# A wait moved: the zero fills of a decode-attention kernel start after the first V load instead of after the output weight

## The chip, the cores, the metric

One core of one Trainium2 chip. The metric is device microseconds (us) of one execution, median over several runs. Times inside an execution are counted from the start of the profiled span, which is about 1.8 us shorter than the device time (763.0 us against 764.8 us).

## The reference

The program is the forward and backward pass of one decode step: layer norm, sliding-window attention over a cache, a gate made by a small MLP, and the gradients of everything. Only the sizes matter here.

```python
B, Sq, D = 2, 1, 512
Hq, Hkv, Sk, Dh = 32, 8, 32768, 128           # the caches are 2 x 8 x 32768 x 128, bf16
W = min(4096, max(256, Sk // 4))              # = 4096: only the last 4096 rows are attended to
k = jnp.repeat(k_cache[:, :, Sk - W:, :], rep, axis=1)
v = jnp.repeat(v_cache[:, :, Sk - W:, :], rep, axis=1)
...
_out, _vjp = jax.vjp(_f, A_x, A_k_cache, A_v_cache, ...)   # returns gradients of the WHOLE caches
```

The gradient of each cache has 32768 rows per head, and 28672 of them are zero. The kernel must write these zeros: 32 heads of 7.3 MB. Together with the 33.6 MB of real gradients, the weights and their gradients, that is 280.5 MB of writes and 45.6 MB of reads.

## The kernel before

The zero fills are DMAs that POOL issues from one tile of zeros (`zt`). They make up 227.6 of 326.7 MB. A fill needs no result, so the kernel is free to choose when fills start; it lets the first one wait for the load of the output weight `wo`.

```python
dma_load = nc.sync            # loads: SP queue
dma_store = nc.scalar         # stores of gradients: ACT queue
...
def zf(o, q, r0, nent, rows, rep=1):          # one zero fill, POOL's queue
    ...
    zs = zt[0:nent * st:st, 0:w].unsqueeze(1).to_broadcast([nent, rep, w])
    sw_fill.append(nc.gpsimd.dma_start(out=v, in_=zs))
    return r0 + nr
...
kvp = attn.enter_context(tc.tile_pool(name="kvp", bufs=1))
w12 = kvp.tile([P, NCB * DH], BF16, tag="k")              # w1 and w2 lie in the tile of K!
w1 = w12[:, 0:DK * F].rearrange("p (k f) -> p k f", k=DK)
w2 = w12[:, DK * F:DK * F + FK * D].rearrange("p (j d) -> p j d", j=FK)
...
def load(src, r, tag):
    nat = kvp.tile([P, NCB * DH], BF16, tag=tag)
    dma_load.dma_start(out=nat[:], in_=kv_of(src, r))     # 4 MB, 32 KB per partition
    return nat[:].rearrange("p (c d) -> p c d", d=DH)
...
    dma_load.dma_start(out=w1, ...)                       # 1.8 MB
    dma_load.dma_start(out=w2, ...)                       # 1.8 MB
    wo_in = dma_load.dma_start(out=wo[:], ...)            # 4 MB
    dma_load.dma_start(out=wq[:], ...)                    # 4 MB
    vnat = load(A_v_cache, 0, "v")                        # V 0
    for qi in range(ZQ - 1):
        ...                                               # 54 fills of 31 heads
    for f in sw_fill:
        tc.add_manual_dep(f.ins, wo_in.ins.name, ...)     # fills wait for wo
    ...                                                   # MLP, transposes of w1, w2, wo; q
knat = load(A_k_cache, 0, "k")                            # K 0: waits until w1, w2 are transposed
for r in range(NR):                                       # 4 rounds: scores, softmax, gradients,
    ...                                                   # store dV, load next V, store dK, load next K
...
with tc.issue_after(last.ins):
    fin = nc.sync.dma_start(out=v, in_=zs)                # the fill of the 32nd head ends the program
```

K 0 shares its tile with `w1` and `w2`, so its load is issued late, when PE has transposed both; and POOL issues its fills in order, so holding back the first holds back all.

Of the kernel before, what the change touches and what calls it, by code (L numbers as in the profile page):

```python
# [16 lines left out]
def kernel(  # L17
# [35 lines left out]
    NJ = N // P  # L53
# [14 lines left out]
    dma_load = nc.sync  # L68
# [21 lines left out]
    def zf(o, q, r0, nent, rows, rep=1):  # L90
        b, hk = divmod(q, HKV)
        nr = nent * rows * rep
        v = o[b, hk, r0:r0 + nr, :]
        w = rows * DH
        if w > ZG * DH:
            v = v.bitcast(F32)
            w //= 2
        v = v.rearrange("(r p g) d -> p r (g d)", p=nent, g=rows)
        st = 4 if nent < 16 else 1
# [3 lines that stand above are left out]
# [71 lines left out]
    wo = wts.tile([P, NJ, D], BF16, name="wo")  # L174
# [29 lines left out]
    def kv_of(t, r):  # L204
        b, h0 = rounds[r]
        return t[b, h0:h0 + NP, SK - W:SK, :].rearrange("h (k c) d -> k h (c d)", c=NCB)

    def load(src, r, tag):
        nat = kvp.tile([P, NCB * DH], BF16, tag=tag)
        dma_load.dma_start(out=nat[:], in_=kv_of(src, r))  # L210
        return nat[:].rearrange("p (c d) -> p c d", d=DH)

    with tc.tile_pool(name="pw", bufs=1) as pw:
# [9 lines left out]
        nc.vector.memset(one_row[:], 1.0)  # L223
        dma_load.dma_start(out=w1, in_=B_w1.rearrange("(p k) f -> p k f", k=DK))
        dma_load.dma_start(out=w2, in_=B_w2.rearrange("(p j) d -> p j d", j=FK))
        wo_in = dma_load.dma_start(out=wo[:], in_=A_wo.rearrange("(p j) m -> p j m", j=NJ))
        dma_load.dma_start(out=wq[:], in_=A_wq.rearrange("(p k) n -> p k n", k=DK))
        vnat = load(A_v_cache, 0, "v")
        for qi in range(ZQ - 1):
            r = 0  # L230
            whole = (P, ZR // P, 1) if qi in zlong else (P, ZG, ZR // (P * ZG))
            for n, rows, rep in zshort.get(qi, (whole,)):
                r = zf(*zparts[qi], r, n, rows, rep)
            assert r == ZR
        for f in sw_fill:
            tc.add_manual_dep(f.ins, wo_in.ins.name,
                              mybir.DependencyInfo(mybir.DependencyClass.Sync, mybir.DependencyReason.DATA))

        tp = ps_m.tile([P, DK, B], BF16, tag="m")
# [65 lines left out]
        for g0 in range(0, len(jobs), 8):  # L305
# [4 lines left out]
            j = 0  # L310
# [10 lines left out]
        for j0 in range(0, NJ, JG):  # L321
            woT = pw.tile([P, JG, DK, P], BF16, tag="woT", bufs=2)
            for half in range(2):
                tp = ps_t.tile([P, 8, P], BF16, tag="pt")
                for jj in range(8):
                    j, dk = divmod(half * 8 + jj, DK)
# [99 lines left out]

    NR = len(rounds)
    knat = load(A_k_cache, 0, "k")
    for r in range(NR):
        nc.vector.tensor_copy(out=zdo[:, :, ZO:ZO + REP], in_=heads(doT_all, r))  # L430
# [110 lines left out]
        if r + 1 < NR:  # L541
            vnat = load(A_v_cache, r + 1, "v")
# [128 lines left out]
```

## Time and profile before

| | before |
|---|---|
| device time, median of 3 (range) | 764.79 us (764.75 to 764.82) |
| profiled span | 763.0 us |
| bytes moved by DMA | 326.73 MB, mean 428 GB/s |
| busy: PE, DVE, ACT, POOL | 52%, 36%, 28%, 4% |
| end of compute; issue of the final fill | 726.7 us; 727.14 us |

The page cuts the span into 40 slices (19.1 us each). Its row DMA is the busy share of the 16 DMA engines in tenths, the row below it what they moved.

```profile
DMA  9999999999999999999999999999999999999998
GB/s 382 439 424 437 410 443 434 435 423 433 419 436 440 419 440 434 427 426 431 431 429 443 431 431 422 432 430 445 426 436 437 431 434 434 415 432 434 421 426 378
DMA packets 10973, 326.73 MB, mean 428 GB/s; under 512 B 2548, under 2 KB 2557, under 8 KB 2586
```

The engines are busy from end to end, and bytes over rate is the span: nothing that compute does matters as long as the engines have something to move. The Trainium skill ("DMA: Bandwidth & Descriptors", Where 436 GB/s comes from) puts the ceiling of the fabric at 435 GB/s; this trace runs at 431 over its long stretch, just below it.

What POOL and SP issue at the start (start, duration, queue, line, transfer; in brackets how long the engine had been idle, and what released it):

```profile
22.88 4.86 POOL L101 DMA_DIRECT2D out_dram<-zt  x8 [21.22 <-DMA wo<-in_A_wo_dram]
```

```profile
2.97 0.61 SPq L210 DMA_DIRECT2D nat<-in_A_v_cache_dram  x1
38.97 0.54 SPq L210 DMA_DIRECT2D nat<-in_A_k_cache_dram  x1
...
726.72 0.33 SPq L635 DMA_DIRECT2D out_dram<-dw  x1
727.14 0.41 SPq L640 DMA_DIRECT2D out_dram<-zt  x1
```

V 0 is queued at once, K 0 only at 38.97 us. The table of stretches gives, for each, the busy time of each engine with counts, then PE's granted clock, the DMA busy share and GB/s, the last column:

```profile
22.00:38.00 16.00, 14.18 (x171) 12.90 (x171) 4.89 (x18) 4.78 (x7) 4.86 (x8) 1.00 1.08 438
38.00:50.00 12.00, 6.93 (x74) 4.68 (x74) 5.69 (x7) 6.24 (x6) 0.00 (x0) 1.00 1.15 429
50.00:100.00 50.00, 39.02 (x364) 22.30 (x363) 19.36 (x33) 19.27 (x19) 1.74 (x3) 0.76 1.05 423
100.00:760.00 660.00, 326.25 (x3424) 191.31 (x3432) 234.37 (x399) 179.99 (x274) 24.33 (x44) 0.65 1.08 431
```

This view does not cut a packet at the edge of a stretch well (a stretch of 4 us can show 508 GB/s), so I use it for 12 us and more. For finer steps I take the trace's packet records and spread each packet's bytes evenly over its duration. From these I also make a sum that the rest leans on, the **lost time**: over steps of 1 us, the sum of (431 - rate) / 431, where 431 GB/s is the rate of the long stretch from 100 to 760 us. It says how many microseconds of full-rate transfer were not used. (The trace's packet records list the packets that a transfer is cut into, each with start, duration, size and queue.)

### The profile page before, as it was taken

Reading aid. Unit: us, or ns where it says so; the run is one execution under the profiler, and the core shown is the slowest. Engines: PE = TensorE matmul, PEld = TensorE weight load, DVE = VectorE, ACT = ScalarE, POOL = GpSimd, SP = SyncE. Lnnn points to the kernel's source line nnn. Section 1 sums busy time; section 2 is a strip of 40 time slices with the busy share of each in tenths; the row PEclk is TensorE's granted clock in tenths of the full one; section 3 lists DMA queues with packets and bytes.
Section 4 is the critical chain, followed back from the end, with each engine's and each line's share of the span. In section 5 each row is a group of like instructions: output and inputs, shape, how many; then the busy total and the mean of one; then the engine's idle time right before and its main releaser. Section 6 shows DMA issues by size and latency. Waiting matters only on the chain.

```text
span 763.0 us, 9422 instructions
## 1 busy us (share of the span) xinstructions
PE 398.6 (52%) x4127; PEld 242.3 (32%) x4136; DVE 274.7 (36%) x481; ACT 216.7 (28%) x314; POOL 32.0 (4%) x63
## 2 busy tenths in 40 slices
PE   5866973853035748640187485002644784866900
PEld 4742552420023534210055341002433443323200
DVE  4334342823012455330054555001324451665600
ACT  3253323523001145430022455000114230721600
POOL 0200000000000100000000000000000000000000
PEclk9986896766558857665579577555767595855555
DMA  9999999999999999999999999999999999999998
GB/s 382 439 424 437 410 443 434 435 423 433 419 436 440 419 440 434 427 426 431 431 429 443 431 431 422 432 430 445 426 436 437 431 434 434 415 432 434 421 426 378
DMA packets 10973, 326.73 MB, mean 428 GB/s; under 512 B 2548, under 2 KB 2557, under 8 KB 2586
## 3 DMA queue, kind: packets, MB, share of 16 engines
q0 software_dynamic: 6784, 227.55, 70.4%
q1 hardware_dynamic: 2696, 56.63, 21.1%
q10 hardware_dynamic: 1452, 41.95, 15.2%
q8 instruction: 32, 0.52, 0.3%
q14 instruction: 9, 0.07, 0.0%
HBM read 45.62 MB, written 280.50 MB: 427 GB/s over the span
## 4 chain that ended last, share of the span: by engine, by line
PE 34%; DMA 33%; DVE 12%; ACT 10%; issue 7%; ACTq 0%; DVEq 0%; SPq 0%
DMA out_dram<-nat 16%; DMA nat<-in_A_k_cache_dram 10%; PE ov L417 7%; PE tp L383 6%; DMA nat<-in_A_v_cache_dram 5%; ACT tring L150 3%; ACT p_bf L451 2%; ACT nat L150 2%; DVE nat L152 2%; PE ps L406 2%; PE s_ps L390 2%; DVE ds_bf L464 2%; PE wps L584 2%; PE dops L331 1%; DVE tring L152 1%
## 5 line engine op out<-in xcount | busy, mean ns | idle before, releaser
L383 PE MATMUL tp<-pperm,nat 128*128 128x128 bf16 x1024 | 93.3, 244 | 178.0 <-DMA nat<-in_A_v_cache_dram 146.1
L152 DVE COPY tring<-tp 128x1024 bf16<-128x1024 bf16 (+1 forms) x98 | 66.3, 689 | 192.1 <-PE tp L383 188.7
L383 PEld LDWEIGHTS <-nat 128*128 128x128 bf16 x1024 | 69.4, 109 | 198.4 <-DMA nat<-in_A_v_cache_dram 148.1
L150 ACT CAST nat<-ov 128x512 bf16<-128x512 f32 x160 | 87.7, 590 | 78.5 <-PE ov L417 57.7
L150 ACT COPY tring<-tp 128x1024 bf16<-128x1024 bf16 (+1 forms) x34 | 34.4, 1011 | 247.6 <-PE tp L383 220.6
L152 DVE CAST nat<-ov 128x512 bf16<-128x512 f32 x96 | 65.7, 690 | 69.3 <-PE ov L417 66.9
L417 PE MATMUL ov<-bd,ds_bf 128*128 128x512 bf16 x124 | 50.0, 483 | 19.0 <-issue 12.9
L101 POOL DMA_DIRECT2D out_dram<-zt x54 | 30.4, 567 | 531.3 <-DMA out_dram<-zt 510.1
L417 PE MATMUL ov<-bd,p_bf 128*128 128x512 bf16 x123 | 46.7, 447 | 5.5 <-ACT nat L150 1.4
L406 PE MATMUL ps<-t,nat 128*128 128x16 bf16 x1024 | 28.8, 173 | 18.2 <-issue 11.4
L406 PEld LDWEIGHTS <-nat 128*128 128x128 bf16 x1024 | 28.7, 103 | 21.1 <-issue 16.0
L152 DVE CAST wq<-wps 128x512 bf16<-128x512 f32 x16 | 11.0, 690 | 54.4 <-PE wps L577 54.2
L390 PEld LDWEIGHTS <-zz 128*32 128x32 bf16 x512 | 17.6, 96 | 33.6 <-issue 23.5
L150 ACT CAST wq<-wps 128x512 bf16<-128x512 f32 x16 | 9.4, 586 | 63.6 <-PE wps L577 63.6
L390 PE MATMUL s_ps<-tring,zz 128*32 128x256 bf16 x256 | 20.0, 301 | 11.2 <-ACT tring L150 7.5
L398 PE MATMUL tp<-ident_bf,p_bf 128*128 128x128 bf16 x64 | 7.5, 310 | 34.9 <-ACT p_bf L451 34.9
L390 PE MATMUL dp_ps<-tring,zz 128*32 128x256 bf16 x256 | 20.0, 319 | 7.4 <-ACT tring L150 5.0
L451 ACT ACTIVATE p_bf<-e_sb,rl 32x512 bf16<-32x512 f32 x16 | 22.8, 1423 | 3.4 <-DVE rl L448 3.3
L417 PEld LDWEIGHTS <-ds_bf 128*128 128x128 bf16 x128 | 13.4, 111 | 27.4 <-issue 25.6
L464 DVE SCALAR_TENSOR_TENSOR ds_bf<-dp_ps,delta,p_bf 32x512 bf16<-32x512 f32 x16 | 21.6, 1352 | 0.2
L417 PEld LDWEIGHTS <-p_bf 128*128 128x128 bf16 x128 | 12.8, 109 | 19.7 <-issue 16.8
L398 PEld LDWEIGHTS <-p_bf 128*128 128x128 bf16 x64 | 6.5, 144 | 35.8 <-ACT p_bf L451 35.8
(198 smaller groups left out, 465.1 us busy)
## 6 DMA issues: line engine op xcount, KB each, us to landing
out_dram<-zt POOLq DMA_DIRECT2D x23, 7168.0 KB, 98.8
out_dram<-nat ACTq DMA_DIRECT2D x8, 4096.0 KB, 41.3
nat<-in_A_v_cache_dram SPq DMA_DIRECT2D x4, 4096.0 KB, 38.4
nat<-in_A_k_cache_dram SPq DMA_DIRECT2D x4, 4096.0 KB, 39.6
out_dram<-zt POOLq DMA_DIRECT2D x2, 7072.0 KB, 68.9
out_dram<-zt POOLq DMA_DIRECT2D x3, 3584.0 KB, 93.2
out_dram<-zt SPq DMA_DIRECT2D x1, 7168.0 KB, 35.0
out_dram<-zt POOLq DMA_DIRECT2D x1, 7104.0 KB, 120.6
```

What stands on the lines that cost most here:

```text
L101: sw_fill.append(nc.gpsimd.dma_start(out=v, in_=zs))
L150: nc.scalar.copy(out=out_ap, in_=in_ap)
L152: nc.vector.tensor_copy(out=out_ap, in_=in_ap)
L331: nc.tensor.matmul(dops[0:B, :, :], lhsT=dsT_bf[:, dk, :], rhs=woT[:, :, dk, :], start=(dk == 0), stop=(dk == DK - 1))
L383: nc.tensor.transpose(tp[:, j, :], nat[:, g * CC + half * CH + j, :], pperm[:].rearrange("p b k -> p (b k)"))
L390: nc.tensor.matmul(out_ps[pr * RB:(pr + 1) * RB, half * CH * PB:(half + 1) * CH * PB], lhsT=zbuf[:, pr, o:o + RB], rhs=tT[:, :, pr, :], st ...
L398: nc.tensor.transpose(tp[:, cc, :], src[:, half * CH + cc].rearrange("r k b -> r (k b)"), ident_bf[:, :])
L406: nc.tensor.matmul(ps[:], lhsT=nat[:, g * CC + half * CH + cc, :], rhs=cols[half][:, cc, :, g, :], start=(half == 0 and g == 0 and cc == 0 ...
L417: nc.tensor.matmul(ov[:], lhsT=src[:, cc].rearrange("r k b -> r (k b)"), rhs=bd[:, gh * 4:(gh + 1) * 4, :], start=True, stop=True)
L451: nc.scalar.activation(out=p_bf[rb, :, :, pr], in_=e_sb[rb], func=ACT.Copy, scale=rl[rb, 0:1])
L464: nc.vector.scalar_tensor_tensor(out=ds_bf[rb, :, :, pr], in0=dp_c[rb], scalar=delta[rb, 0:1], in1=p_bf[rb, :, :, pr], op0=ALU.subtract, o ...
L584: nc.tensor.matmul(wps[:], lhsT=o_rows[:, j:N:NJ], rhs=ds_rows[:, :], start=True, stop=True)
```

## The change

Hold the fills back until V 0 has landed. The intent: in the first stage the loads get the engines to themselves, so V 0 is there earlier. No instruction is added, removed or reordered; the listing of both programs engine by engine differs in the one semaphore that POOL's first fill waits for.

```diff
+    kv_loads = []
+
     def load(src, r, tag):
         nat = kvp.tile([P, NCB * DH], BF16, tag=tag)
-        dma_load.dma_start(out=nat[:], in_=kv_of(src, r))
+        kv_loads.append(dma_load.dma_start(out=nat[:], in_=kv_of(src, r)))
         return nat[:].rearrange("p (c d) -> p c d", d=DH)
@@
-        wo_in = dma_load.dma_start(out=wo[:], in_=A_wo.rearrange("(p j) m -> p j m", j=NJ))
+        dma_load.dma_start(out=wo[:], in_=A_wo.rearrange("(p j) m -> p j m", j=NJ))
@@
         for f in sw_fill:
-            tc.add_manual_dep(f.ins, wo_in.ins.name,
+            tc.add_manual_dep(f.ins, kv_loads[0].ins.name,
                               mybir.DependencyInfo(mybir.DependencyClass.Sync, mybir.DependencyReason.DATA))
```

## The prediction

> **What bounds the kernel now.** The DMA engines. The page's queue table sums to 326.73 MB and the DMA row of its slices shows 9 tenths in 39 of 40 slices, mean 428 GB/s: bytes over rate is the whole 763.0 us span. The trace's packet records, summed per 20 us, give 428 to 433 GB/s from 2 us to 762 us without a hole. The Trainium skill ("DMA: Bandwidth & Descriptors", Where 436 GB/s comes from) gives a ceiling of 435 GB/s; the trace agrees. PE is busy 52%, DVE 36%, ACT 28%. Compute ends at 726.7 us; the last 35 us are stores of the output weight and the last zero fill (issued 727.14, landed 35.0 us later).
>
> **What the change does.** No instruction is added, removed or reordered; the programs' listings differ in one wait of POOL: the first fill waits for V load 0 instead of wo. Before, wo landed at 22.1 us, the first fill was issued at 22.88 us, and its first packet ran at 27.1 us. V load 0 landed at 50.8 us, sharing the engines with fills (packets of 57,344 bytes against its 32,768). Now the loads have the engines alone: w1, w2, wo, wq and V are 16.25 MB, which at 431 GB/s plus 1.7 us of start (an estimate) land at 40 to 41 us, 10 us sooner. Fills are issued then; their first packets run near 45 us, 18 us later than now.
>
> **How much is on the critical path.** Almost nothing.
> - The engines should not run dry at the hand-over. The load of K 0 waits for the transposes of w1 and w2 (last at 38.7 us) and is issued at 38.97 us, its first packet 0.2 us later. So K 0 (4.19 MB, 9.7 us alone) is queued 1 to 2 us before V drains and covers the 5 us until the first fill packet.
> - Earlier V, wq and K buy nothing: V is first read at 86.4 us, wq at 74 us, and before 155 us PE waits for no DMA but x and w1 (2.2 and 5.9 us). This stage is paced by PE, ACT and DVE; the first store of dV stays at 153 us.
> - The queues share the engines without losing throughput ("DMA: Bandwidth & Descriptors", Issuing engines are not separate DMA queues). Fills postponed by 18 us are caught up by 86 us, when K 0 has landed in both: the same bytes have then moved, and the rest finds the same backlog. The fills still end near 728 us.
>
> Reads alone ran at 433 GB/s, mixed with fills at 430: 18 us of that saves 0.1 us. Hand-over holes cost 0 to 1 us.
>
> **Prediction.** 764.9 us, range 763.9 to 766.4. Faster by over 2%: 0.01; within: 0.97; slower: 0.02.
>
> **What would show each step.** First fill issued at 40 to 42 us; issue to landing of V 0 near 38 us rather than 47.8; K 0 landed near 60 us rather than 86, still issued at 39 us; first store of dV near 153 us; DMA at 428 GB/s or more between 40 and 50 us; last software fill packet within 2 us of 728.5; final fill issued near 727. Bytes unchanged.
>
> **What would make it wrong.** K 0 issued later or slow to start, so that the engines idle until fill descriptors arrive: up to 5 us lost. Or the fills' odd sizes, apparently tuned to balance the 16 engines, fall beside other transfers and leave single engines idle at the end: 1 to 3 us. Or later loads meet a different mix and delay the compute end past what 15 us of queued stores cover.

## The result

| | before | changed |
|---|---|---|
| device time, median of 6 (range) | 764.88 us (764.75 to 765.04) | 766.93 us (766.02 to 768.00) |
| ratio, 95% interval | 1 | 1.0026 (1.0014 to 1.0039) |
| profiled span | 763.0 us | 766.2 us |
| first fill issued by POOL | 22.88 us | 43.15 us |
| K 0 issued by SP | 38.97 us | 38.95 us |
| end of compute (issue of the store of dw1) | 726.72 us | 711.02 us |
| lost time, 10 to 100 us | 0.35 us | 1.85 us |
| lost time, 100 to 760 us | -0.28 us | -0.15 us |
| lost time of the uneven end (from 758 us to the last packet) | 0.85 us | 2.40 us |

A ratio is the mean time of one kernel's fast runs over that of the other's of the same rounds, so it is not quite the ratio of the medians quoted. The change is slower by 2.05 us (0.26%), clear of the interval though well within 2%. The profiled run is the slowest of the six (768.0 us); the others' spans were 764.2 to 765.3 us.

The slices of the page after:

```profile
DMA  9999999999999999999999999999999999999998
GB/s 384 431 388 436 420 444 423 441 420 434 434 422 436 422 446 429 430 426 437 424 427 438 435 427 433 431 430 438 438 429 435 426 427 420 437 441 417 440 416 344
DMA packets 10973, 326.73 MB, mean 426 GB/s; under 512 B 2548, under 2 KB 2557, under 8 KB 2586
```

Same packets, same bytes. The **third** slice (38 to 57 us) has fallen from 424 to 388 GB/s, and the last from 378 to 344. Note that the busy share still reads 9 in the third slice. POOL, SP and the stretches after (lines of the file are two higher than before):

```profile
43.15 4.84 POOL L101 DMA_DIRECT2D out_dram<-zt  x8 [41.50 <-DMA nat<-in_A_v_cache_dram]
```

```profile
2.81 0.60 SPq L212 DMA_DIRECT2D nat<-in_A_v_cache_dram  x1
38.95 0.54 SPq L212 DMA_DIRECT2D nat<-in_A_k_cache_dram  x1
...
711.02 0.33 SPq L637 DMA_DIRECT2D out_dram<-dw  x1
713.63 0.39 SPq L642 DMA_DIRECT2D out_dram<-zt  x1
```

```profile
22.00:38.00 16.00, 14.28 (x166) 12.94 (x167) 4.84 (x17) 5.06 (x7) 0.00 (x0) 1.00 1.02 436
38.00:50.00 12.00, 8.35 (x72) 5.58 (x72) 4.83 (x6) 5.96 (x5) 4.84 (x8) 0.86 0.99 374
50.00:100.00 50.00, 37.40 (x389) 22.31 (x389) 20.93 (x35) 20.03 (x20) 1.73 (x3) 0.86 1.19 426
100.00:760.00 660.00, 322.53 (x3409) 186.89 (x3408) 233.33 (x397) 179.15 (x274) 24.25 (x44) 0.66 1.07 431
```

From 38 to 50 us the busy share is 0.99 and the engines move 374 GB/s instead of 429; from 100 us on both run at 431. The share sums the times of all packets, the 4-byte ones that end a transfer included, so it can exceed 1 (1.15 before) and does not say that every engine is at work. GB/s in steps of 1 us, from the packet records:

```
us       38  39  40  41  42  43  44  45  46  47  48  49
before  422 436 427 433 431 427 439 431 429 431 436 432
changed 433 421 294 309 366 385 368 339 299 322 391 432
```

The records also show how many packets are under way. With loads alone it is 16.0 or 16.1 in every step from 28 to 39 us of the changed run, one for each of the 16 engines, so a number below 16 means engines without work (4-byte packets left out; "again" is the second profile told of below):

```
us         38   39   40   41   42   43   44   45   46   47   48   49
before   16.0 16.6 16.2 16.4 16.4 16.1 16.4 16.3 16.2 16.1 16.4 16.3
changed  16.0 15.6 12.2 14.6 15.2 16.0 16.0 16.0 15.6 16.0 16.0 16.0
again    16.0 16.0  8.2 11.4 16.0 16.0 16.0 16.1 16.1 16.0 16.1 16.0
```

So there are two different losses. From 40 to 43 us engines do stand empty: V 0 ended on its 16 engines at 39.8 to 42.1 us, and K 0's first packet ran at about 40.3 us, 1.3 us after its issue began (records do not name the transfer; I tell K 0's packets by their length). The empty places make 0.40 of the 0.77 us lost from 39 to 43 us, and 0.78 of 1.07 us in the second profile. The rest is slow packets: V 0's of 32,768 bytes take 1.21 us each until 40 us; those that began between 40.3 and 41.3 us took 1.57 us on average, up to 1.93. From 43 to 48 us nearly all places are filled, and the packets are slow. The first packet of a fill ran at 47.95 us, and by 49 us the rate was back.

The sums close: 1.50 us more lost from 10 to 100 us and 1.55 us more at the uneven end make 3.05 us; the last packet ended 3.24 us later (765.00 against 761.76 us). That is book-keeping (the bytes are the same): it shows where time was lost. What it does not tell is why K 0 ran slowly, and whether the uneven end is a consequence or a second cause. For there is a rival: in the changed run compute ended 15.7 us earlier, the final fill was issued at 713.6 us instead of 727.1, and it mixed with other fills.

### The profile page after: what moved, and what is told of

It is laid out like the page before. It is cut to its first block, busy times and chain, and to the rows that moved or that the text cites. A ratio compares the mean times of both kernels' runs of the same rounds, so it can differ in the third digit from the quotient of the medians.

```text
span 766.2 us, 9431 instructions
## 1 busy us (share of the span) xinstructions
PE 395.2 (52%) x4136; PEld 239.2 (31%) x4136; DVE 274.3 (36%) x481; ACT 216.6 (28%) x314; POOL 31.9 (4%) x63
## 4 chain that ended last, share of the span: by engine, by line
PE 33%; DMA 32%; DVE 12%; ACT 10%; issue 6%; ACTq 0%; DVEq 0%; SPq 0%
DMA out_dram<-nat 17%; DMA nat<-in_A_v_cache_dram 9%; PE tp L385 6%; PE ov L419 6%; DMA nat<-in_A_k_cache_dram 5%; ACT tring L150 3%; ACT p_bf L453 2%; DVE tring L152 2%; ACT nat L150 2%; DVE ds_bf L466 2%; PE s_ps L392 2%; DVE nat L152 2%; PE wps L586 2%; PE ps L408 1%; PE dops L333 1%
## 5 line engine op out<-in xcount | busy, mean ns | idle before, releaser
L385 PE MATMUL tp<-pperm,nat 128*128 128x128 bf16 x1024 | 88.9, 237 | 167.3 <-DMA nat<-in_A_v_cache_dram 151.9
L385 PEld LDWEIGHTS <-nat 128*128 128x128 bf16 x1024 | 65.8, 106 | 186.6 <-DMA nat<-in_A_v_cache_dram 153.7
L419 PE MATMUL ov<-bd,p_bf 128*128 128x512 bf16 x128 | 49.5, 460 | 4.1 <-DVE nat L152 1.4
L408 PEld LDWEIGHTS <-nat 128*128 128x128 bf16 x1024 | 28.6, 102 | 20.1 <-issue 15.0
L392 PE MATMUL s_ps<-tring,zz 128*32 128x256 bf16 x256 | 19.3, 290 | 12.2 <-ACT tring L150 7.6
```

Of the source, the lines that this page charges most:

```text
L385: nc.tensor.transpose(tp[:, j, :], nat[:, g * CC + half * CH + j, :], pperm[:].rearrange("p b k -> p (b k)"))
L392: nc.tensor.matmul(out_ps[pr * RB:(pr + 1) * RB, half * CH * PB:(half + 1) * CH * PB], lhsT=zbuf[:, pr, o:o + RB], rhs=tT[:, :, pr, :], st ...
L408: nc.tensor.matmul(ps[:], lhsT=nat[:, g * CC + half * CH + cc, :], rhs=cols[half][:, cc, :, g, :], start=(half == 0 and g == 0 and cc == 0 ...
L419: nc.tensor.matmul(ov[:], lhsT=src[:, cc].rearrange("r k b -> r (k b)"), rhs=bd[:, gh * 4:(gh + 1) * 4, :], start=True, stop=True)
```

## The experiments

Theory A: the loss is made at 39 to 49 us, where K 0 is alone in the queues. Theory B: it is made at the end, because the first stage is lightened, compute ends early, the final fill starts early and the engines end unevenly. Later theories appear where they came up. Medians of before are those of the same rounds (9 or 11 runs); the others have 5 runs, or 6 where said. Every kernel gave correct results.

### Fills wait for wq, which lands between wo and V 0

```diff
-            tc.add_manual_dep(f.ins, kv_loads[0].ins.name,
+            tc.add_manual_dep(f.ins, wq_in.ins.name,
```

> All fills wait for wq (lands near 31 us) in place of V 0. Theory A (the loss of about 2 us is made at 39 to 49 us, where the load of K 0 is alone in the queues and does not run the engines at 431 GB/s): here V 0 and then fill packets (from about 36 us) lie beside the start of K 0, so there is no hole at 39 to 43 us; 764.8 to 765.3 us, 0 to 0.4 us over before. Theory B (the loss is made at the end, because compute ends some 15 us earlier, the final fill is issued early and mixes with the software fills, and the 16 engines end unevenly): the stage before is lightened nearly as much as in the change, compute ends early too, and the time is 766 to 767 us. Sub-question: if POOL's burst of eight issues slows any load (A1), the packets of V 0 at 32 to 36 us take 1.3 to 1.5 us instead of 1.213.

Measured: 764.61 us (764.51 to 764.73) against 764.79 (764.69 to 764.95); ratio 0.9997 (0.9985 to 1.0009). POOL's first issue was at 33.26 us, its first packet at 37.20. Lost from 39 to 49 us: nothing (-0.05 us); a small dip at 34 to 39 us (0.33 us). So holding fills back by 10 us costs nothing, as A said. But compute ended at 724 us here, so B, which hangs on an early end of compute, is not excluded by it; my claim that compute would end early was wrong.

### One early fill, the rest after V 0

```diff
-        for f in sw_fill:
-            tc.add_manual_dep(f.ins, kv_loads[0].ins.name,
+        for n, f in enumerate(sw_fill):
+            tc.add_manual_dep(f.ins, (wq_in if n == 0 else kv_loads[0]).ins.name,
```

> Only the first fill waits for wq, all others for V 0 as in the change. The first fill (7.3 MB) covers the hand-over from V 0 to K 0. Theory A: the hole at 39 to 49 us is gone or below a quarter (under 0.5 us of lost bytes), time 764.8 to 765.4 us. Theory B: compute ends as early as in the change, so 766 to 767.5 us. If a burst of POOL issues slowed packets even beside other traffic, packets of V 0 or K 0 at the burst would take longer than 1.255 us.

Measured: 764.60 us (764.43 to 764.67) against 764.79; ratio 0.9997 (0.9985 to 1.0009). A single fill of 7.3 MB beside the hand-over from V 0 to K 0 removes the whole loss: lost from 10 to 100 us 0.17 us. It does two things that this run does not separate: it runs beside the hand-over, and by sharing the engines it puts the end of V 0 off to 46.6 to 50.3 us, so that K 0 (issued at 39.00 us) is queued over 7 us ahead. The stretches say the same as before the change:

```profile
38.00:50.00 12.00, 6.79 (x76) 4.61 (x74) 5.58 (x7) 6.28 (x6) 0.00 (x0) 1.00 1.17 427
```

### One fill after V 0, the rest after K 0

Is it POOL's burst of eight issues (from 43.15 us, 4.84 us long) that slows K 0? Here POOL issues one.

```diff
+        for n, f in enumerate(sw_fill):
+            tc.add_manual_dep(f.ins, kv_loads[min(n, 1)].ins.name, ...
```

(The fills move in the text to below the load of K 0; POOL's order is unchanged.)

> The first fill waits for V 0 as in the change, the others for K 0, so POOL issues one fill instead of eight while K 0 is alone (43 to 48 us). A1 (the burst of issues slows the packets of K 0): the packets that start at 44 to 48 us take 1.22 us, and the loss falls from 1.9 us to about 0.9 us: time 765.6 to 766.2 us. A2 (K 0 alone is slow by itself, whatever POOL does): packets there still take 1.4 to 1.7 us, time as the change, 766.5 to 767.5 us. B: as the change.

Measured: 769.73 us (768.86 to 771.08) against 764.79; ratio 1.0064 (1.0051 to 1.0077). A miss of mine: the single fill was used up at about 68 us, before the other fills were issued at 71.68 us, so a hole of four microseconds opened there (176, 60, 27, 1, 66 GB/s in the steps from 68 us). What the run was made for can still be read: with one issue instead of eight, the steps from 43 us read 399, 400, 373, 320, 350 and 393 GB/s; lost from 43 to 49 us 0.82 us, against 1.12 us in the change and 0.75 us in its second profile. The number of issues makes no difference: A1 as I put it (the burst) falls.

### All fills after K 0

```diff
-            tc.add_manual_dep(f.ins, kv_loads[0].ins.name,
+            tc.add_manual_dep(f.ins, kv_loads[1].ins.name,
```

(Here too the fills move in the text to below the load of K 0.)

> All fills wait for K 0, so K 0 has the engines alone to its end (about 50 us) and POOL issues nothing meanwhile. A1: after its first packets (1.4 to 1.9 us each at 40 to 42 us) K 0 runs at 1.213 us per packet and lands near 50.5 us; then a real hole of about 5 us with no packet; time before + 0.8 + 5, about 770.5 us. A2: K 0 stays at 1.4 to 1.7 us per packet and lands at 52 us or later; about 772 us. B: the time follows the end of the engines only, a hole here shows as less than its length if the end was uneven.

Measured (6 runs): 769.75 us (767.92 to 772.13) against 764.79; ratio 1.0066 (1.0053 to 1.0079). Now K 0 is alone to its end and POOL issues nothing until 55.12 us:

```profile
55.12 4.83 POOL L101 DMA_DIRECT2D out_dram<-zt  x8 [53.48 <-DMA nat<-in_A_k_cache_dram]
```

```
us       38  39  40  41  42  43  44  45  46  47  48  49
fill_k  433 428 276 296 368 394 385 385 414 426 432 433
```

K 0 is slow from 40 to about 46 us with no help from POOL, and then runs at full rate, still alone, with packets of 1.21 us. So being alone is not what slows it: its **start** does, and costs 1.18 us (39 to 49 us), 0.51 us of it in empty places (11.5, 13.6 and 15.0 packets under way from 40 us). That is neither A1 nor A2 as I had put them. Then comes the real hole of five microseconds that was expected. Lost time closes again: 5.92 us from 10 to 100 us, 5.57 more than before, and the last packet 5.85 us later. Compute ended here at 713.9 us, as early as in the change, the final fill was issued at 716.25 us, and yet the end was as even as before (0.97 us lost there, 0.85 before). That speaks against B. One more reading for later: with the engines empty, the first packet of a fill came at 56.37 us, 1.25 us after POOL's issue began, and took 2.13 us, as later ones do.

### The changed kernel again

> The changed kernel once more, beside the others of this call, for a second profile. Theory A (refined: K 0 is issued about 1 us before the queue drains, its start is slow, POOL's first fill slows it further, and the engine that loses most sets the end): packets of K 0 at 40 to 48 us take 1.3 to 1.8 us, about 1.5 to 2 us of lost bytes, median time 766 to 767.2 us; and the largest loss of one engine between 33 and 48 us, less 0.3, matches the span over 763.0 to within 0.7 us. Theory B (uneven end because the final fill is issued early): the span follows the spread of the last packets and not the loss at 39 to 49 us.

Measured: 766.54 us (765.80 to 767.06) against 764.94 (764.74 to 765.13); ratio 1.0021 (1.0009 to 1.0034). In this profile compute ended at 729.0 us, not early at all, and the final fill was issued at 729.42 us; the kernel was as slow as ever. **B is dead** as the cause of the loss, and the 15.7 us that compute seemed to gain are a difference between runs. The dip is there again (218, 250, 362 GB/s from 40 us; 1.79 us lost from 10 to 100). K 0 was issued at 39.54 us here, V 0 ended on its engines from 40.0 us on, K 0's first packet ran at about 40.9 us, and half of the places stood empty meanwhile. Over the same 12 us the busy share now shows it, though not how much:

```profile
38.00:50.00 12.00, 8.72 (x77) 5.92 (x75) 4.71 (x6) 6.42 (x6) 4.83 (x8) 0.78 0.92 358
```

The end was nearly even this time, 0.95 us lost, and the span 764.6 us: 1.44 + 0.10 = 1.54 us, and the last packet 1.61 us later. My attempt to predict the span from the engine that lost most failed: following packets from end to start gave the worst engine no smaller a loss here than in the first profile, where the excess was twice as large. Records do not name the engine, and where packets end together that chaining is unsafe.

### K 0 and V 0 exchanged

```diff
-    w12 = kvp.tile([P, NCB * DH], BF16, tag="k")
+    w12 = kvp.tile([P, NCB * DH], BF16, tag="v")
@@
-        vnat = load(A_v_cache, 0, "v")
+        knat = load(A_k_cache, 0, "k")
@@
-    knat = load(A_k_cache, 0, "k")
+    vnat = load(A_v_cache, 0, "v")
```

> As the change, but K 0 is loaded in the first row of loads and V 0 after the transposes of w1 and w2, each into its own tile; fills wait for K 0. Theory A (the place in the queue makes the load slow): V 0 now has the slow packets, mean 1.3 to 1.45 us over all, K 0 1.213 to 1.23 us; time 766 to 767.5 us. Rival (something about K: its source or its tile): the second load runs at 1.213 us and the time falls to 764.8 to 765.3 us.

Measured: 766.88 us (765.81 to 768.02) against 764.94; ratio 1.0021 (1.0007 to 1.0035). V 0, now the second, has the slow start (246, 229, 270, 332 GB/s from 40 us, with 9.9, 11.4, 12.2 and 13.8 packets under way), K 0 runs at 1.22 us a packet. It is the place in the queue, not the data or the tile. The final fill was issued at 729.73 us here, and 1.92 us were lost at the end all the same: an uneven end does not need an early final fill, which B had assumed.

### Fills wait for w2, earlier than before

```diff
-            tc.add_manual_dep(f.ins, kv_loads[0].ins.name,
+            tc.add_manual_dep(f.ins, w2_in.ins.name,
```

> All fills wait for w2 (lands near 12 us), earlier than before. Theory A: loads of wo, wq and V 0 are queued behind each other when POOL starts, so only POOL's first issue costs, 0.3 us, as before: 764.6 to 765.2 us. If more sharing at the start cost throughput, or compute became late enough to leave the engines dry at the end (wo lands later, near 30 us): 765.5 to 768 us.

Measured: 764.76 us (764.63 to 764.86) against 764.94; ratio 0.9998 (0.9985 to 1.0010). From w2 (POOL issues at 13 us) over wo to wq (33 us) the start of the fills does not matter; only past that does it cost.

### A cover on the SP queue

If K 0's start is slow because the queue has just run low, then something queued well ahead should help. Half of the first fill moves to the SP queue, behind V 0 and ahead of K 0.

```diff
+        b, hk = divmod(zparts[0][1], HKV)
+        half = P * ZG
+        dma_load.dma_start(out=out_2[b, hk, 0:half, :].rearrange("(r p g) d -> p r (g d)", p=P, g=ZG // 2),
+                           in_=zt[:].bitcast(BF16).unsqueeze(1).to_broadcast([P, 2, ZG * DH // 2]))
+        zf(*zparts[0], half, P, ZG, 1)
-        for qi in range(ZQ - 1):
+        for qi in range(1, ZQ - 1):
```

> As the change, but half of the first fill (3.67 MB) moves from POOL to the SP queue, behind V 0 and ahead of K 0, so that the engines have a queued transfer at the hand-over and K 0 starts behind it. All POOL fills still wait for V 0. Theory A: no rate below 400 GB/s at 39 to 43 us; what is left is POOL's first issue, 0.3 us; time 764.7 to 765.4 us. Theory A with POOL's first issue as the main cost: 765.5 to 766.2 us. Theory B (the late wait lightens the first stage, compute ends early and the end is uneven): as the change, 766 to 767.5 us.

Measured: 766.51 us (766.11 to 766.79) against 764.94; ratio 1.0020 (1.0008 to 1.0033). A miss: the dip was still there (402, 315, 261, 354, 418 GB/s from 38 us), though the half fill had been queued at 8.12 us and K 0, which began near 50 us, started without a dip. This time it was the last packets of V 0 that were slow (2.07 us on average at 39 us, with all 16 places filled). Either the loads are slowed by something that happens near 40 us in any case, or there is a second loss where the engines turn from loads to the first stores.

### K 0 in three pieces

The transfer of K 0 is cut so that 5 us of it are queued behind V 0 in time; nothing else changes, neither compute nor the bytes.

```diff
         vnat = load(A_v_cache, 0, "v")
+        dma_load.dma_start(out=w12[:, DK * F + FK * D:NCB * DH], in_=kv_of(A_k_cache, 0)[:, :, DK * F + FK * D:NCB * DH])
@@
-    knat = load(A_k_cache, 0, "k")
+    dma_load.dma_start(out=w12[:, 0:DK * F], in_=kv_of(A_k_cache, 0)[:, :, 0:DK * F])
+    dma_load.dma_start(out=w12[:, DK * F:DK * F + FK * D], in_=kv_of(A_k_cache, 0)[:, :, DK * F:DK * F + FK * D])
+    knat = w12[:].rearrange("p (c d) -> p c d", d=DH)
```

> As the change, but the load of K 0 is cut into three transfers, each issued as soon as its bytes of the shared tile are free: 0.5 MB with the first loads, 1.8 MB when w1 has been transposed (about 28 us), 1.8 MB when w2 has been (about 39 us). So 5 us of K 0 are queued behind V 0 before V 0 ends. Late-start theory (a load that is issued when the queue is nearly empty starts slowly): no rate below 400 GB/s at 39 to 43 us, what is left is POOL's first issue (0.3 to 0.8 us near 45 us); time 765.0 to 765.7 us. Time-locked theory (the engines' loads are slowed near 38 to 42 us by whatever goes on there, as half of the fill queued well ahead did not help): rate of 250 to 350 GB/s at 39 to 43 us as in the change, 766 to 767.2 us. If the issue of a transfer slows loads that are under way, a dip shows near 28 to 31 us as well.

Measured: 765.69 us (765.44 to 765.85) against 764.92 (764.79 to 765.10); ratio 1.0010 (0.9998 to 1.0022). The pieces were issued at 8.12, 27.68 and 38.88 us.

```
us         38  39  40  41  42  43  44  45  46  47  48  49
k_pieces  433 432 425 420 425 426 409 321 281 333 419 437
```

The dip at 39 to 43 us is gone (0.05 us lost, 0.77 in the change; never fewer than 16.0 packets under way): K 0's late start is one half of the loss. What is left is at 43 to 49 us (0.92 us), just before and as the first fill packets come (first at 47.73 us): K 0's packets of 14,336 bytes took 0.83 us at 45 us instead of 0.54. No dip followed the issue at 27.68 us, so issuing a transfer does not slow those under way.

### The cover ahead of V 0

The same half fill as above, but between wq and V 0. Then the turn from loads to a store comes at about 31 us, far from K 0's issue, and V 0 has the engines alone from 40 us.

```diff
+        dma_load.dma_start(out=out_2[b, hk, 0:half, :]. ...)      # as above, one line higher
         vnat = load(A_v_cache, 0, "v")
```

> Half of the first fill on the SP queue again, but ahead of V 0 instead of behind it, so V 0 runs from about 40 to 49 us, K 0 is queued 10 us before V 0 ends, and POOL's fills start near 50 us. Turn theory (engines that go from loads to stores, or to a new transfer after the loads, lose time at the turn): a dip at 30 to 34 us (wq to fill), perhaps a second at 39 us (fill to V 0), none at 49 us. Time-locked theory (K 0's issue at 39 us, or compute at that time): dip at 38 to 42 us, none at 30 to 34 us. Time 765.3 to 766.8 us in both.

Measured (6 runs): 766.42 us (765.93 to 771.08; without the one slow outlier, which nothing explains, to 766.63) against 764.92; ratio 1.0031 (1.0013 to 1.0050), which that outlier pulls up.

```
us               26  27  28  29  30  31  32  33 ..  38  39  40  41  42  43
sp_cover_early  430 433 415 352 265 332 414 428    430 429 431 433 433 434
```

The stretches of the profile show it too, the loss now in the row from 22 us:

```profile
22.00:38.00 16.00, 13.93 (x167) 12.64 (x167) 5.16 (x18) 5.03 (x8) 0.00 (x0) 1.00 0.99 400
38.00:50.00 12.00, 7.29 (x76) 4.76 (x75) 5.58 (x6) 5.95 (x6) 0.00 (x0) 1.00 1.04 447
```

The dip has moved with the turn from loads to the store, 0.9 us in all (wq's last packets took 2.02 us at 29 us), and at 38 to 43 us there is none, although K 0 is issued and compute runs there as always. Nothing time-locked, then. The change back from the store to V 0 at 39 us costs nothing, nor does K 0 behind V 0 near 50 us, queued 10 us ahead. And POOL's eight issues, from 53.39 us on, lie beside a load that runs alone at 425 to 433 GB/s: the issues themselves slow nothing, which settles A1.

That loads turn to stores is not enough, though. In this same profile they do so a second time, at 57.26 us, when POOL's first fill begins beside K 0 after some 14 us of loads alone: 0.01 us lost from 50 to 60 us. What cost time in every version were the first stores of the execution, where they came beside loads. This second turn was seen in one profile only.

### Both edits that helped

> The two edits that each took loss away, together: the first fill waits for wq and the others for V 0, and K 0 is loaded in three pieces. If the late start of K 0 and the turn from loads to fills are all that differs between the versions, nothing is left to gain over the first edit alone: 764.4 to 764.8 us, within 0.1% of before. A time under 764.2 us would show a loss in before that was not seen; over 765 us that the smaller packets of K 0 (14,336 bytes) cost something beside fills.

```diff
+            tc.add_manual_dep(f.ins, (wq_in if n == 0 else kv_loads[0]).ins.name,   # as in the second experiment
+        dma_load.dma_start(out=w12[:, ...], in_=kv_of(A_k_cache, 0)[:, :, ...])     # three pieces, as above
```

Measured: 765.36 us (765.05 to 765.65) against 764.86 (764.73 to 765.02); ratio 1.0006 (0.9992 to 1.0019). A small miss: 0.5 us above before, where the one early fill alone was 0.2 below. Lost from 10 to 100 us 0.45 us. (The interval contains 1, but all five runs lie above all nine of before.) Why pieces cost half a microsecond beside fills stays open.

### The ledger

Lost time in us, as defined above, from the packet records of one profiled run each. "End" is the loss from 758 us to the last packet.

| kernel | 10 to 100 us | of it 39 to 43 | of it 43 to 49 | 100 to 760 us | end | last packet ended |
|---|---|---|---|---|---|---|
| before | 0.35 | -0.01 | -0.02 | -0.28 | 0.85 | 761.76 |
| changed | 1.85 | 0.77 | 1.12 | -0.15 | 2.40 | 765.00 |
| changed, again | 1.79 | 1.07 | 0.75 | -0.31 | 0.95 | 763.37 |
| K and V exchanged | 2.47 | 1.28 | 1.27 | -0.29 | 1.92 | 765.01 |
| fills after w2 | 0.51 | 0.01 | -0.02 | -0.27 | 0.77 | 761.82 |
| fills after wq | 0.30 | -0.01 | -0.04 | -0.24 | 0.83 | 761.62 |
| one after wq, rest V 0 | 0.17 | -0.01 | -0.03 | -0.26 | 0.62 | 761.38 |
| one after V 0, rest K 0 | 5.48 | 0.49 | 0.82 | -0.20 | 1.09 | 767.20 |
| fills after K 0 | 5.92 | 0.83 | 0.35 | -0.19 | 0.97 | 767.61 |
| cover behind V 0 | 1.03 | 0.87 | 0.00 | -0.30 | 1.70 | 763.34 |
| cover ahead of V 0 | 0.83 | -0.01 | -0.03 | -0.28 | 1.28 | 762.72 |
| K 0 in pieces | 0.97 | 0.05 | 0.92 | -0.32 | 0.80 | 762.29 |
| pieces and one early fill | 0.45 | -0.01 | -0.02 | -0.24 | 0.94 | 761.98 |

In every row the last packet's excess over before is the excess of the columns "10 to 100" and "end" to within 0.2 us. From 100 to 760 us all versions are alike to 0.2 us: whatever was lost early is never made up later.

## Why the prediction was wrong, point by point

- **What bounds the kernel**: right. 431 GB/s from 100 to 760 us in both; every microsecond of lost transfer came out at the end, and the compute end did not set the time: profiles with compute ending at 711.0 us (the change) and at 729.3 us (K and V exchanged) both spanned 766 us.
- **The step that failed**: "The engines should not run dry at the hand-over ... So K 0 (4.19 MB, 9.7 us alone) is queued 1 to 2 us before V drains and covers the 5 us until the first fill packet." K 0 was issued when I said (38.95 us) and V 0 ended about when I said, but the engines did run partly dry. I had counted "its first packet 0.2 us later"; that packet, at 39.18 us in the trace of before, was the first of V 0 (the 257th of 32,768 bytes; wo and wq have 256), for wq was still being loaded. K 0's first packet came 1.3 us after its issue (1.3 us in three more profiles: the second of the change, K and V exchanged, fills after K 0), when engines had begun to finish V 0 (39.8 to 42.1 us), and only 12.2 of 16 places were filled from 40 to 41 us, 8.2 in the second profile. Moreover I took a queued transfer to be a transfer at full rate, and where all places were filled the packets were slow. From 39 to 49 us the engines ran at 349 GB/s on average (the mean of the ten steps), not 431. The term "Hand-over holes cost 0 to 1 us" measured 1.5 us in lost bytes, and with the uneven end 1.6 to 3.2 us of span. I had named the risk ("K 0 issued later or slow to start") but given it no weight in the sum.
- **Its two halves**: the late start of K 0, which was issued about a microsecond before V 0 began to end (0.8 to 1.1 us at 39 to 43 us in the two profiles; gone when K 0 was queued in pieces), and the first stores beside loads (0.9 us with the pieces, 0.9 us with the cover ahead of V 0). Before, the first stores cost only about 0.3 us and the late start nothing: V 0 ended there at 63.7 to 67.5 us, so K 0 had been queued 25 us ahead, and fills ran beside both.
- **The uneven end**: not foreseen in this form. I had named the odd sizes of the fills as what might leave engines idle at the end. The change's second profile lost only 0.95 us there and was still slow, so the end is not what makes the change slow in every run. The versions whose lost time at 28 to 49 us did not end in a hole lost 0.8 to 2.4 us at the end, those without such a dip 0.6 to 0.9 us, those with a hole afterwards 1.0 and 1.1 us. An explanation that fits is that engines lose unequally, and each has a fixed share of bytes, while a hole lets them line up again. It is argued, not shown: the records do not name the engine.
- **"Earlier V, wq and K buy nothing"**: right. V 0 landed earlier and the time did not fall.
- **"Fills postponed by 18 us are caught up by 86 us"**: right but for the lost bytes; from 100 us on the traces agree.
- **A misreading**: V 0 before did not land at 50.8 us. The 47.8 us from issue to landing that I read belong to K 0 (38.97 + 47.8 = 86.8 us); the view had a landing for only one of the two transfers that write that tile. V 0 before ended on its engines at 63.7 to 67.5 us. This one did not enter the sum; the 0.2 us told of above did.
- **The listed signs**: K 0 issued at 39 us (38.95), bytes unchanged: right. First fill issued at 40 to 42 us: 43.15. Landing of V 0 about 38 us after its issue: 40.3 (2.81 to 43.15 us). K 0 landed near 60 us: 71.8 (38.95 + 32.8 us). Last packet of the software fills within 2 us of 728.5: 744.8 in the first profile, 728.1 in the second. "DMA at 428 GB/s or more between 40 and 50 us": wrong, and the one that mattered. The signs at the end (first store of dV 147.8 us instead of 153, final fill 713.6 instead of 727) missed in the first profile; the final fill was within 2.5 us of 727 in the second (729.42).

What stays open: why the first packets of a transfer issued so late are slow even where all 16 places are filled; why the first stores cost 0.2 to 0.4 us in some versions and 0.9 in others; the half microsecond of the pieces beside an early fill.

No version clearly beats the kernel before. One fill after wq and the rest after V 0, or all after wq, ran at 764.6 us, 0.2 us under before in nearly every run, but the interval (0.9985 to 1.0009) contains 1.

## What to carry to other kernels

In a kernel that is bound by DMA, look at GB/s and at the packets under way, not at the busy share: a share of 0.99 went with 374 of 429 GB/s here. A transfer that is queued about a microsecond before the queue drains does not cover the gap (its first packet came 1.3 us after its issue); have another stream under way across every hand-over (one early 7.3 MB fill was enough), or queue the next transfer well ahead (10 us was enough with the cover ahead of V 0). And before making others wait so that a load may come sooner, ask whether anyone waits for that load: here nobody did.

## What the Trainium skill lacked or had wrong

- "DMA: Bandwidth & Descriptors", Rules for kernel authors, asks for 128 partitions and at least 1 MiB per DMA for maximum bandwidth. K 0 is 4 MB over 128 partitions and still ran at 276 to 414 GB/s for its first 7 us when its queue had nearly drained (1.18 us lost where nothing else ran beside it). No page says how far ahead a transfer has to be queued: about 1 us was too short here, 10 us was enough (cover ahead of V 0). The first load of the program shows the cost of a start too: 0.77 to 0.92 us lost from 2 to 10 us in every version.
- No page says that the first stores beside loads cost time: 0.9 us lost when half a fill followed the loads on the same queue, 0.2 to 0.4 us when POOL's first fill came at 17 to 37 us (before, and fills after w2 or wq), 0.9 us when it came near 48 us with K 0 in pieces, and nothing at a second turn from loads to stores.
- "DMA: Bandwidth & Descriptors", Specifications, gives about 1 us to the first byte of a DMA from GpSimd. With the engines empty that is about right: 1.25 us from the start of POOL's first issue to the first packet (55.12 to 56.37 us, fills after K 0). With loads under way it was 3.9 to 5.2 us: 4.2 before (22.88 to 27.10 us), 4.8 in the changed kernel (43.15 to 47.95 us).
- The same page, Issuing engines are not separate DMA queues, says that DMAs started by different engines run on the same 16 DMA engines and interleave. The runs agree: loads, stores and fills from three queues made 431 GB/s together, no more than loads from one queue alone (433).
